# Half-width rotation tables and coefficients folded into them, in a fused state-space and MLP kernel

## The chip, the cores and the metric

The kernel runs on one core of a Trainium2 chip. The metric is device time in microseconds (us) of one execution. Below, PE is the matmul engine, PEld its weight load, DVE the vector engine, ACT the scalar engine, POOL the general-purpose engine and SP the engine that issues most DMAs. All profiled executions named here were of state fast.

## The reference, cut to what matters

The input x is 2048 rows of 1024. Two branches are computed from it and mixed by a gate per row:

```
g = sigmoid((x * gate_w).sum(-1))
# branch a: a diagonal complex state-space model with 1024 states
Lam_bar = exp(dt * Lam);  B_bar = ((Lam_bar - 1) / Lam)[:, None] * B
Bu = x @ B_bar^T
h[t] = Lam_bar * h[t-1] + Bu[t]          # 2048 steps
a = 2 * real(h @ C^T) + x * Dskip
# branch b: layer norm, 1024 -> 3584, gelu, 3584 -> 1024
out = g * a + (1 - g) * b
```

## The kernel before: the parts that matter

The rows come in 8 chunks of TP = 256; the states in 8 groups of 128. For each chunk and state group there is one *scan unit*, 64 in all. PE makes z = B x (L777). DVE rotates z by -theta*j ("pre"), runs two real scans with the decay r, and rotates back by +theta*j ("post"). With the rotation taken out, the complex recurrence is two real ones. The tables cos(theta*j) and sin(theta*j) are 256 wide, built once; j counts from 0 in each chunk, and the state is rotated by theta*256 between chunks.

```python
def s_unit_dve(c, pc):                      # A, B, Cv, Dv, E: fp32 tiles of 128x256
    # pre: six tensor_tensors, A = zre*cos + zim*sin, Cv = zim*cos - zre*sin
    tensor_tensor_scan(A, rb, A, init_re, mult, add)
    tensor_tensor_scan(Cv, rb, Cv, init_im, mult, add)
    # post: six tensor_tensors, h_re = A*cos - Cv*sin, h_im = A*sin + Cv*cos, to bf16
```

The factor (Lam_bar-1)/Lam of B_bar is a complex number per state. The kernel before multiplies it into C, while it transposes C by PE in 16 blocks during the first chunk:

```python
def tc_block(pc, dh):
    ...  # 8 PE transposes into one PSUM bank: creT, cimT
    K.op("act", ... activation(kt0, cimT, Identity, scale=k1b))
    K.op("act", ... activation(kt1, cimT, Identity, scale=k2b))
    STT(k1, creT, k1a, kt0, mult, add)      # DVE, 128x512, L459
    STT(k2, creT, k1b, kt1, mult, add)
```

SBUF is the memory that the engines work in, PSUM the one that PE writes to, in banks. STT below is a scalar_tensor_tensor, one DVE instruction that does two operations. w1 and w2 are the weights of the two MLP layers: w1 is loaded by SP, 1 MB at a time, into two buffers; w2 by POOL in eight loads of 0.9 MB, four for each half of its columns. bt is the transposed B.

So there are two stages. In the *start*, chunk 0 goes through its scan units and the first MLP layer in eight rounds; tables are built, B and C transposed, weights loaded. Then each chunk's second MLP layer and output are woven with the next chunk's scan units and first MLP layer (the *steady state*). The first second-layer matmul, L870, marks the border.

## Time and profile before

The time was 709.8 us (median of 4, 708.98 to 711.25). The next fence is the busy time of each engine in four stretches: start and length in us, busy us of each engine (instructions), then the granted PE clock, the DMA share and GB/s.

```profile
20.00:60.00 40.00, 31.50 (x299) 26.79 (x297) 32.05 (x78) 32.86 (x64) 28.66 (x60) 0.85 0.83 264
60.00:95.00 35.00, 23.74 (x229) 19.58 (x230) 32.56 (x73) 27.13 (x47) 6.03 (x12) 0.90 0.86 293
160.00:240.00 80.00, 79.04 (x566) 53.85 (x564) 56.68 (x151) 22.22 (x40) 38.52 (x56) 1.00 0.55 179
240.00:320.00 80.00, 79.03 (x564) 53.66 (x562) 53.18 (x151) 22.67 (x41) 35.16 (x53) 1.00 0.55 180
```

The columns are PE, PEld, DVE, ACT, POOL. In the steady state PE is busy 79 of 80 us and DVE 53 to 57: PE is the limit. In the start, PE is busy 31.5 of 40 and 23.7 of 35 us; from 60 to 95 us DVE is busy 32.6 of 35.

The chain of waits of the first 112 us, by line, names DVE first:

```profile
by line: DVE ct L459 16.7%; DVE vt L442 12.8%; issue 6.2%; PE psF L777 6.1%; DMA arena<-in_A_log_dt_dram 5.0%; PE psF L835 4.7%; DVE vt L461 3.2%; ACT arena L767 2.7%; PE psF L870 2.6%; ACT arena L769 2.6%; POOL arena L452 2.5%; DVE vt L803
```

DVE's timeline around one scan unit shows costs (start us, duration us, instruction):

```profile
61.42 1.40 DVE L459 SCALAR_TENSOR_TENSOR ct<-psF,cs,arena 128x512 bf16<-128x512 bf16 x2
62.74 1.40 DVE L459 SCALAR_TENSOR_TENSOR ct<-psT,cs,arena 128x512 bf16<-128x512 bf16 x2
64.06 0.41 DVE L442 TENSOR_TENSOR vt<-psF,tabc 128x256 f32<-128x256 f32 x1
...
65.38 0.75 DVE L442 TENSOR_TENSOR vt<-vt 128x256 f32<-128x256 f32 x2
66.05 0.75 DVE L803 TENSOR_TENSOR_SCAN vt<-cs,vt 128x256 f32<-128x256 f32 x1
66.71 0.73 DVE L805 TENSOR_TENSOR_SCAN vt<-cs,vt 128x256 f32<-128x256 f32 x1
67.35 0.40 DVE L442 TENSOR_TENSOR vt<-vt,tabc 128x256 f32<-128x256 f32 x1
```

Recorded durations overlap, so costs are read from start to start. An STT takes 0.66 us ((64.06 - 61.42)/4), a scan 0.66 us, a tensor_tensor 0.33 us. The pre part begins at 64.06, the scans at 66.05, the post part at 67.35: the scans take 1.30 us.

### The profile page before, as it was taken

To read this page: it belongs to the slowest core of one execution; us is meant where nothing else is said; L and a number is where in the kernel's file an instruction comes from. 1 tells how busy PE (TensorE), PEld (TensorE's weight loads), DVE (VectorE), ACT (ScalarE), POOL (GpSimd) and SP (SyncE) were. 2 spreads that over 40 slices of the span, in tenths; PEclk is the share of its full clock that TensorE was granted. 3 is DMA by queue.
4 is the path that set the end of the run, shared out by engine and by line. 5 is a ranking of instruction groups with operands and counts; after the bars stand their busy time and mean duration, and the time that the engine had idled before them with its cause. 6 is when DMAs were issued, how large, how long until landed. Compare 5 with 4: busy or idle time off the path is not lost.

```text
span 709.4 us, 12210 instructions
## 1 busy us (share of the span) xinstructions
PE 658.6 (93%) x4738; PEld 449.2 (63%) x4738; DVE 459.9 (65%) x1228; ACT 234.0 (33%) x416; POOL 331.2 (47%) x509
## 2 busy tenths in 40 slices
PE   4878669999999999999999999999999999999994
PEld 3666546666666666666666666666666666666541
DVE  3789896777677666575677667575677666555300
ACT  6787962222322232212312232222312232211100
POOL 5681343655353644354353643364353642443573
PEclk9889998999999999999999999999999999999998
DMA  7786989466554646356554656355554655462220
GB/s 267 253 282 207 322 287 329 157 190 208 179 168 140 228 152 220 133 183 204 179 182 136 216 168 212 129 191 194 178 194 136 212 174 170 144 190 91 60 51 16
DMA packets 84627, 130.04 MB, mean 183 GB/s; under 512 B 4890, under 2 KB 66330, under 8 KB 84570
## 3 DMA queue, kind: packets, MB, share of 16 engines
q1 hardware_dynamic: 76330, 104.88, 45.1%
q0 software_dynamic: 8240, 24.39, 10.9%
q8 instruction: 37, 0.61, 0.4%
q14 instruction: 20, 0.16, 0.1%
HBM read 120.86 MB, written 8.39 MB: 182 GB/s over the span
## 4 chain that ended last, share of the span: by engine, by line
PE 82%; DVE 7%; ACT 5%; POOL 2%; issue 1%; DMA 1%; DVEq 0%; POOLq 0%; ACTq 0%
PE psF L870 27%; PE psF L835 25%; PE psF L885 15%; PE psF L777 15%; DVE ct L459 3%; DVE vt L442 2%; ACT xT L714 2%; DMA arena<-in_A_log_dt_dram 1%; PE psT L711 1%; ACT hid L838 1%; DVE vt L461 1%; ACT arena L767 0%; ACT arena L769 0%; POOL arena L452 0%; DVE vt L803 0%
## 5 line engine op out<-in xcount | busy, mean ns | idle before, releaser
L835 PE MATMUL psF<-yT,w1s 128*128 128x256 bf16 x1792 | 235.0, 276 | 5.7 <-ACT hid L838 3.0
L835 PEld LDWEIGHTS psF<-yT,w1s 128*128 128x128 bf16 x1792 | 176.6, 99 | 64.6 <-ACT hid L838 4.1
L442 POOL TENSOR_TENSOR arena<-arena 128x512 f32<-128x512 f32 (+1 forms) x96 | 120.0, 1250 | 143.3 <-ACT arena L877 101.1
L442 DVE TENSOR_TENSOR vt<-psF,tabc 128x256 f32<-128x256 f32 x128 | 53.6, 419 | 182.3 <-PE psF L777 180.3
L777 PE MATMUL psF<-xT,bts 128*128 128x256 bf16 x1024 | 129.7, 276 | 1.7 <-ACT bts L733 1.1
L838 ACT ACTIVATE arena<-psF,b1c 128x256 bf16<-128x256 f32 x112 | 53.1, 474 | 226.8 <-PE psF L835 226.8
L777 PEld LDWEIGHTS psF<-xT,bts 128*128 128x128 bf16 x1024 | 100.9, 99 | 27.8 <-ACT bts L733 1.5
L870 PE MATMUL psF<-w2s,hid 128*128 128x512 bf16 x448 | 110.6, 381 | 1.5 <-ACT xT L714 1.5
L838 ACT ACTIVATE hid<-psF,b1c 128x256 bf16<-128x256 f32 x112 | 52.0, 478 | 170.4 <-PE psF L835 170.4
L870 PE MATMUL psF<-w2s,arena 128*128 128x512 bf16 x448 | 107.1, 379 | 0.0
L870 PEld LDWEIGHTS psF<-w2s,arena 128*128 128x128 bf16 x448 | 43.7, 98 | 39.8
L870 PEld LDWEIGHTS psF<-w2s,hid 128*128 128x128 bf16 x448 | 43.8, 98 | 37.6 <-ACT xT L714 1.6
L885 PE MATMUL psF<-ct,hT 128*128 128x512 bf16 x256 | 63.1, 379 | 0.0
L452 POOL TENSOR_SCALAR lnf<-lnf 128x1 f32<-128x1 f32 x32 | 17.5, 547 | 96.9 <-DVE lnf L678 95.2
L885 PE MATMUL psF<-ct,arena 128*128 128x512 bf16 x256 | 61.8, 379 | 0.0
L896 POOL DMA_DIRECT2D out_dram<-arena x32 | 17.5, 548 | 93.2 <-DVE arena L459 65.4
L442 DVE TENSOR_TENSOR vt<-vt,tabc 128x256 f32<-128x256 f32 x128 | 53.9, 421 | 0.0
L442 DVE TENSOR_TENSOR vt<-psF,tabs 128x256 f32<-128x256 f32 x128 | 53.1, 415 | 0.0
L442 DVE TENSOR_TENSOR vt<-vt 128x256 f32<-128x256 f32 x128 | 52.5, 452 | 0.0
L442 DVE TENSOR_TENSOR vt<-vt,tabs 128x256 f32<-128x256 f32 x128 | 49.9, 431 | 0.0
L803 DVE TENSOR_TENSOR_SCAN vt<-cs,vt 128x256 f32<-128x256 f32 x64 | 49.3, 771 | 0.0
L459 DVE SCALAR_TENSOR_TENSOR arena<-psF,gall,arena 128x512 bf16<-128x512 f32 x32 | 23.9, 746 | 37.0 <-PE psF L885 35.6
(111 smaller groups left out, 647.0 us busy)
## 6 DMA issues: line engine op xcount, KB each, us to landing
w1s<-in_B_w_dram SPq DMA_DIRECT2D x56, 1024.0 KB, 5.8
bts<-bt_scratch SPq DMA_DIRECT2D x56, 512.0 KB, 3.6
w2s<-in_B_w_dram POOLq DMA_DIRECT2D x8, 896.0 KB, 10.0
xn<-in_A_x_dram SPq DMA_DIRECT2D x16, 256.0 KB, 6.1
bt_scratch<-bts SPq DMA_DIRECT2D x8, 512.0 KB, 3.2
arena<-in_A_x_dram POOLq DMA_DIRECT2D x32, 128.0 KB, 3.7
arena<-in_A_Dskip_dram POOLq DMA_DIRECT2D x32, 128.0 KB, 3.8
arena<-in_B_b_dram POOLq DMA_DIRECT2D x32, 128.0 KB, 3.9
```

The source lines that it names most:

```text
L442: K.op(eng, lambda e: e.tensor_tensor(out_, a, b, op), reads=r, writes=w, name=name, after=after)
L452: K.op(eng, lambda e: e.tensor_scalar(out_, a, s1, s2, op0, op1), reads=r, writes=w, name=name, after=after)
L459: K.op(eng, lambda e: e.scalar_tensor_tensor(out_, a, s, b, op0, op1), reads=r, writes=w, name=name, after=after)
L461: K.op(eng, lambda e: e.scalar_tensor_tensor(out_, a, s, b, op0, op1, accum_out=accum), reads=r, writes=w, name=name, after=after)
L714: K.op("act", lambda e: e.activation(dst[:, :, s * TB:(s + 1) * TB], bap[:, 0:NDC, :], AF.Identity), reads=[bkey], writes=[dkey], name="tr ...
L777: K.op("pe", lambda e, ri=ri, dc=dc: e.matmul(psF[:, PZ, ri * TP:(ri + 1) * TP], bts[:, slot, dc, ri * 128:(ri + 1) * 128], xT[:, dc, :], ...
L803: K.op("dve", lambda e: e.tensor_tensor_scan(A, rb, A, Cc("init_re", pc), ALU.mult, ALU.add), reads=[kv(VA), kc("r"), kc("init_re")], writ ...
L835: K.op("pe", lambda e, dc=dc: e.matmul(psF[:, ab, 0:TP], w1s[:, slot, dc, fl * 128:(fl + 1) * 128], yT[:, dc, :], start=(dc == 0), stop=(d ...
L838: K.op("act", lambda e: e.activation(hid[hb][:, fc, :], psF[:, ab, 0:TP], AF.Gelu_apprx_tanh, bias=b1c[:, fc:fc + 1]), reads=[kps(ab), ("b ...
L870: K.op("pe", lambda e, fc=fc: e.matmul(psF[:, PM, 0:DH], hid[hb][:, fc, tbl * TB:(tbl + 1) * TB], w2s[:, fc, dh * DH:(dh + 1) * DH], start ...
L885: K.op("pe", lambda e, k=k: e.matmul(psF[:, PS_, 0:DH], hT[hb][:, k, tbl * TB:(tbl + 1) * TB], ct[:, k, dh * DH:(dh + 1) * DH], start=(k = ...
L896: K.dma("pool", lambda e: e.dma_start(out2[tbg * TB:(tbg + 1) * TB, dh * DH:(dh + 1) * DH], ost[:, 0, :]), reads=[("ost", 0)], name="out_s ...
```

## The change

Its intent: multiply the factor not into C but into the post tables (16 tables of 128 columns instead of scaling 16 blocks of C), so that C needs plain copies only. The post tables need room. So the tables shrink to T = 128, used twice per chunk by a stride-0 dimension; the scan is split in two, and the state is rotated by theta*128 at the join. The coefficients are now needed before the first unit ends, so their computation moves forward. Two DMA issues move too: the first-half w2 loads, all in the fifth round before, go one each into rounds 2 to 5, and the reloads of transposed B (bt prefetch) go to the end of a round.

```diff
-    T = TP
+    T = 128
+    NF = TP // T
@@ scan unit
+            for f in range(NF):
+                ... scan a_f, scan c_f, each 128 wide
+                if f + 1 < NF:          # four 128x1 operations on DVE
+                    TS("dve", t1, c_l, sT, mult);  TS("dve", t2, c_l, cT, mult)
+                    STT(mre, a_l, cT, t1, mult, subtract);  STT(mim, a_l, sT, t2, mult, add)
-            TT("dve", B, A, tc_, ALU.mult, ...)        # post with the plain tables
+            TT("dve", B, A, pcn, ALU.mult, ...)        # post with tables that hold the factor
@@ C blocks
-            two ACTIVATEs with scale, two STTs
+            two plain copies of 128x512: even blocks on ACT, odd ones on DVE
@@ new
+        def ptable(pc, eng):            # POOL: six 128x128 operations for each group
+            tpc = k1a*cos + k1b*sin;  tpn = k2b*sin + k1b*cos
@@ order
+        consts_dve_2(); consts_act(); coef_chain()     # moved ahead of the first unit
+            if 1 <= rnd < 1 + NW2G:
+                w2_load(rnd - 1, 0)                    # POOL queue, before the round's ptable
+            for pcc in fin_batches.get(rnd, []):
+                ptable(pcc, "pool")
+            if rnd == 0:
+                for pc in pool_tabs[2:]:
+                    table_pool_args(pc)                # arguments of tables 4 to 7
-            if rnd == w2a_round:                       # round 5 (counting from 1)
-                for g in range(NW2G):
-                    w2_load(g, 0)
+            if pcn < NPC:
+                bt_prefetch(pcn + 3)                   # was right after s_unit_dve
```

## The prediction

> **What bounds it now.** The kernel has two stages. The 40-slice page shows PE at 9 tenths from slice 7 on; the busy-by-stretch table gives PE 79.04 of every 80 us between 160 and 640 us. There one 256-row chunk takes 79.5 us and is PE-bound; DVE is busy 54 of 80 us, off the critical path. The start, up to the first second-layer matmul (L870) at 104.56 us, is different: between 20 and 106 us PE is busy 61.9, ACT 66.6, DVE 75.4 of 86 us, and from 38 us DVE hardly idles. The chain of waits walks there mostly over DVE: the C-coefficient STTs (L459, 16.7% of the first 112 us) and the scan unit's tensor_tensors (L442, 12.8%).
>
> **What the change removes.** In the start only: 32 STTs of 128x512 (0.66 us from start to start, 21 us) on DVE and 32 scaling ACTIVATEs (0.57 us, 18 us), as the coefficients move from C into the "post" tables. 128-wide tables also halve table elements on ACT and POOL.
>
> **What it adds.** 32 plain copies, half on ACT (about 0.57 us each, 9 us), half on DVE. For these I estimate 0.35 to 0.65 us, 6 to 10 us: the Trainium skill's "VectorE: DVE Perf Modes", section "The perf-mode tier table", allows a PSUM copy up to 2x, which no run so far shows. POOL builds 8 post tables, 6 operations of 128x128 each, about 2 us by its 0.41 to 0.73 us for 128x256. In each of the 64 scan units two 256-wide scans (0.66 us) become four 128-wide ones (estimate 0.36 us) plus four 128x1 rotations in a dependent chain (0.07 to 0.2 us each, by the other tiny DVE operations): about +0.8 us a unit, 5.6 to 6.4 us. The stride-0 table operands I take as free (0.33 us per tensor_tensor as now).
>
> **What lies on the critical path.** Steady state: DVE rises from 54 to about 60 of 80 us, still below PE; expected cost about 0. Start: DVE net -21 + 8 + 6.4, some -6 us, and the waits of DVE for ACT (4.98 us at 33 us, 0.85, 1.5) mostly go. The coefficient chain moves ahead of the first table: the second layer norm waits for POOL, so the first unit's end and the second table come 2 to 3 us later; but the third unit starts about 36 to 37 us instead of 42.2. Following the rounds, the last unit of chunk 0 begins about 88 us instead of 99.8. Earlier w2 loads and the later bt prefetch also take a 2.6 us w1 wait of PE at 92 us away. Against it: DMA, busy 0.85 of 20 to 106 us at 278 GB/s, must deliver the same bytes sooner, and ACT becomes nearly as busy as DVE. I discount to a gain of 11 us, all before the first L870.
>
> **Time:** 698.5 us, range 691 to 705. Faster by over 2% 0.28, within 2% 0.68, slower 0.04.
>
> **What would show it.** First L870 matmul at about 93 us (90 to 99) instead of 104.6; from there to the end unchanged, about 605 us, chunk period 79.5 us; DVE in 240 to 320 us at 59 to 62 us instead of 53; 128-wide scans at 0.45 us recorded or less; third unit's first "pre" near 37 us; PE waits for DVE (L459) inside the start gone.
>
> **What would make it wrong.** Scans or rotations costing so much that DVE nears 80 us a chunk (then slower); broadcast operands running slower; the early coefficient chain delaying the first MLP matmuls by more than 4 us; DMA or ACT table loads (1.28 us, two per second round) becoming the limit of the start (gain 4 us or less); or, the other way, PE becoming the limit and the gain reaching 15 us or more.

## The result

The kernel after takes 700.46 us (median of 10, 699.59 to 701.45); the kernel before 710.05 us (median of 15). The ratio is 0.9865, 95% interval 0.9852 to 0.9878. Ratios here are the mean time of one kernel's fast runs over that of the other's fast runs of the same rounds, so they are not quite the ratios of the medians quoted.

The same four stretches after:

```profile
20.00:60.00 40.00, 34.55 (x362) 29.48 (x362) 32.43 (x99) 33.42 (x61) 30.79 (x73) 0.92 0.88 297
60.00:95.00 35.00, 24.26 (x244) 20.97 (x242) 31.20 (x90) 20.45 (x40) 22.97 (x52) 0.90 1.01 342
160.00:240.00 80.00, 79.03 (x564) 53.65 (x562) 65.46 (x197) 22.65 (x41) 36.76 (x55) 1.00 0.58 182
240.00:320.00 80.00, 79.04 (x565) 53.79 (x564) 65.51 (x198) 22.26 (x41) 35.51 (x53) 1.00 0.57 178
```

PE in the steady state is unchanged; DVE rose from 53 to 65.5 us and stays under PE. From 60 to 95 us POOL's work went from 6 to 23 us and the DMA share from 0.86 to 1.01.

The border of the stages, from PE's timeline, first before and then after:

```profile
104.56 1.89 PE L870 MATMUL psF<-w2s,hid 128*128 128x512 bf16 x4 [1.48 <-ACT xT L714]
```

```profile
94.94 1.89 PE L918 MATMUL psF<-w2s,hid 128*128 128x512 bf16 x4 [1.48 <-ACT xT L742]
```

The start became 9.6 us shorter (104.56 - 94.94). From there to the end of the span it takes 604.8 us before (709.4 - 104.56) and 603.6 after (698.5 - 94.94), and the transposes that end each chunk come 79.51 us apart in both traces. The gain lies in the start.

DVE's timeline around one unit after, with the same columns as before:

```profile
68.84 0.74 DVE L795 COPY ct<-psF 128x512 bf16<-128x512 bf16 x2
69.51 0.74 DVE L795 COPY ct<-psT 128x512 bf16<-128x512 bf16 x2
70.17 0.41 DVE L445 TENSOR_TENSOR vt<-psF,tabc 128x256 f32<-128x256 f32 x1
...
72.16 0.48 DVE L840 TENSOR_TENSOR_SCAN vt<-cs,vt 128x128 f32<-128x128 f32 x1
72.55 0.46 DVE L842 TENSOR_TENSOR_SCAN vt<-cs,vt 128x128 f32<-128x128 f32 x1
73.04 0.34 DVE L453 TENSOR_SCALAR mfx<-vt,cs 128x1 f32<-128x1 f32 x2
73.30 0.34 DVE L462 SCALAR_TENSOR_TENSOR mfx<-vt,cs,mfx 128x1 f32<-128x1 f32 x2
73.67 0.48 DVE L840 TENSOR_TENSOR_SCAN vt<-cs,mfx,vt 128x128 f32<-128x128 f32 x1
74.08 0.46 DVE L842 TENSOR_TENSOR_SCAN vt<-cs,mfx,vt 128x128 f32<-128x128 f32 x1
74.45 0.40 DVE L445 TENSOR_TENSOR vt<-vt,tpc 128x256 f32<-128x256 f32 x1
```

A copy takes 0.33 us ((70.17 - 68.84)/4) where an STT took 0.66. The scans and the join take 2.29 us (74.45 - 72.16) where they took 1.30: 1.0 us more a unit. The broadcast table operand is free: 0.33 us from start to start as before.

The chain of waits of the first 112 us no longer names the STTs; it names a w1 load:

```profile
by line: DMA w1s<-in_B_w_dram 10.3%; DVE vt L445 7.6%; ACT bts L761 6.6%; PE psF L918 6.3%; PE psF L883 5.6%; POOL cs L445 5.4%; issue 4.5%; ACT hid L886 4.1%; DMA arena<-in_A_log_dt_dram 3.9%; PE psF L801 3.7%; DVE vt L464 3.3%; ACT L886 2
```

This is a single load, issued at 34.11 us and landed 11.56 us later. It is not new: in the kernel before, one issued at 33.95 took 11.81 us, and was not on the chain.

There is a new wait. In the fifth unit DVE stands still until POOL has built that unit's post table. The timeline of 56 to 72 us, cut to the lines that show it:

```profile
58.42 0.29 POOL L455 TENSOR_SCALAR tabc<-tabc 128x128 f32<-128x128 f32 x1
58.66 1.96 POOL L537 DMA_DIRECT2D w2s<-in_B_w_dram  x2
60.66 0.38 POOL L455 TENSOR_SCALAR arena<-tabc,cs 128x128 f32<-128x128 f32 x1
...
62.82 0.45 POOL L445 TENSOR_TENSOR tpn<-arena 128x128 f32<-128x128 f32 x1
63.38 0.42 DVE L445 TENSOR_TENSOR vt<-vt,tpc 128x256 f32<-128x256 f32 x1 [5.30 <-POOL tpn L445]
...
69.73 1.01 PE L758 MATMUL psF<-ident,arena 128*128 128x128 bf16 x8 [5.63 <-DVE ct L795]
```

The brackets give the idle time before an instruction and what ended it. POOL's queue was in order: the arguments of tables 4 to 7, two w2 issues, then the post table of group 4. DVE lost 5.30 us, and PE 5.63 us behind it, because the copies that free the transposes' PSUM banks came late on DVE.

### The profile page after: what moved, and what is told of

It reads as the page before. It is cut to its first block, busy times and chain, and to the rows that moved or that the text cites. A ratio compares the mean times of both kernels' runs of the same rounds, so it can differ in the third digit from the quotient of the medians.

```text
span 698.5 us, 12590 instructions
## 1 busy us (share of the span) xinstructions
PE 654.7 (94%) x4738; PEld 447.4 (64%) x4738; DVE 527.1 (75%) x1596; ACT 220.7 (32%) x400; POOL 338.3 (48%) x557
## 4 chain that ended last, share of the span: by engine, by line
PE 83%; ACT 6%; DVE 4%; POOL 2%; DMA 2%; issue 1%; SPq 1%; POOLq 0%; DVEq 0%; ACTq 0%
PE psF L918 28%; PE psF L883 25%; PE psF L933 15%; PE psF L801 14%; ACT xT L742 2%; DMA w1s<-in_B_w_dram 2%; DVE vt L445 1%; ACT bts L761 1%; POOL cs L445 1%; ACT hid L886 1%; DMA arena<-in_A_log_dt_dram 1%; PE psT L739 1%; DVE vt L464 1%; ACT L886 0%; DVE ct L795 0%
## 5 line engine op out<-in xcount | busy, mean ns | idle before, releaser
L883 PE MATMUL psF<-yT,w1s 128*128 128x256 bf16 x1792 | 231.4, 273 | 3.4 <-ACT hid L886 1.9
L801 PE MATMUL psF<-xT,bts 128*128 128x256 bf16 x1024 | 131.4, 279 | 0.3 <-ACT bts L761 0.3
L445 DVE TENSOR_TENSOR vt<-vt 128x256 f32<-128x256 f32 x128 | 71.6, 600 | 0.0
L455 POOL TENSOR_SCALAR lnf<-lnf 128x1 f32<-128x1 f32 x32 | 17.4, 543 | 89.1 <-DVE lnf L706 87.5
L445 DVE TENSOR_TENSOR vt<-vt,tpc 128x256 f32<-128x256 f32 x128 | 53.6, 419 | 6.1 <-POOL tpn L445 6.1
L445 DVE TENSOR_TENSOR vt<-vt,tpn 128x256 f32<-128x256 f32 x128 | 48.8, 423 | 0.0
L455 POOL TENSOR_SCALAR arena<-arena,gall 128x512 f32<-128x512 bf16 x64 | 45.9, 723 | 2.4 <-DMA arena<-in_B_b_dram 2.4
```

The source lines that it names most:

```text
L445: K.op(eng, lambda e: e.tensor_tensor(out_, a, b, op), reads=r, writes=w, name=name, after=after)
L455: K.op(eng, lambda e: e.tensor_scalar(out_, a, s1, s2, op0, op1), reads=r, writes=w, name=name, after=after)
L801: K.op("pe", lambda e, ri=ri, dc=dc: e.matmul(psF[:, PZ, ri * TP:(ri + 1) * TP], bts[:, slot, dc, ri * 128:(ri + 1) * 128], xT[:, dc, :], ...
L883: K.op("pe", lambda e, dc=dc: e.matmul(psF[:, ab, 0:TP], w1s[:, slot, dc, fl * 128:(fl + 1) * 128], yT[:, dc, :], start=(dc == 0), stop=(d ...
```

## The experiments

The theory with which they began: the start is bound by DVE's work, folding takes 21 us of STTs out of it, the split costs 1.0 us in each of its 8 units, and the moved DMA issues are a detail. The rivals: the narrower tables give the gain; the moved DMA issues give it; something other than DVE sets the start's pace.

Twelve kernels ran. Two of them, fold_only and pool_first_fold, leave out the rotation at the join and so are wrong (they serve for timing and say nothing of the result); w2_double loads one matrix twice and is still correct, like all others. The table below collects the times. "Before" of each row is the kernel before in the same rounds.

| kernel | us, median | before, us | ratio, 95% interval | first second-layer matmul, us | from there to the end, us |
|---|---|---|---|---|---|
| before | 709.8 | | | 104.56 | 604.8 |
| after | 700.46 | 710.05 | 0.9865 (0.9852 to 0.9878) | 94.94 | 603.6 |
| split_only | 708.2 | 709.0 | 0.9982 (0.9957 to 1.0008) | 101.59 | 604.6 |
| fold_only | 701.11 | 709.0 | 0.9887 (0.9858 to 0.9915) | 96.39 | 604.0 |
| old_order | 707.7 | 709.0 | 0.9982 (0.9951 to 1.0013) | 93.74 | 610.6 |
| new_order | 710.05 | 709.0 | 1.0013 (0.9986 to 1.0041) | 103.51 | 604.4 |
| split_new_order | 708.7 | 709.38 | 0.9986 (0.9971 to 1.0001) | 102.37 | 602.9 |
| pool_first | 698.88 | 709.38 | 0.9854 (0.9837 to 0.9870) | 92.41 | 602.9 |
| pool_first_ln | 700.94 | 709.38 | 0.9876 (0.9850 to 0.9902) | 92.62 | 607.1 |
| pool_first_fold | 698.03 | 709.38 | 0.9841 (0.9826 to 0.9856) | 93.34 | 604.1 |
| w2_early | 696.94 | 710.3 | 0.9804 (0.9789 to 0.9819) | 92.68 | 602.0 |
| w2_early_ln | 698.0 | 710.3 | 0.9833 (0.9808 to 0.9857) | 91.69 | 603.8 |
| w2_double | 704.74 | 710.3 | 0.9917 (0.9902 to 0.9932) | 99.71 | 603.1 |
| tile_64 | 775.88 | 710.3 | 1.0898 (1.0864 to 1.0932) | 98.49 | 676.2 |

The last two columns come from one profiled execution each (the last is span minus the column before it). Its first unit begins anywhere from 14.69 us (new_order) to 18.55 us (w2_double), so one or two us in the border are chance.

### split_only: the half-width tables and split scans without the folding

```diff
 (to the kernel before)
+ T = 128, NF = 2; split scans with the join; consts_dve_2 and consts_act ahead of the first table
  C is still scaled by 2 ACTIVATEs and 2 STTs a block; w2 loads and bt prefetch as before
```

> The kernel before with 128-wide tables and split scans (the sines of the constants are computed earlier, as the split needs), but with C still scaled by 32 ACTIVATEs and 32 STTs. Theory (the gain comes from the DVE work that folding the coefficients removes from the start; the split is a cost that only the PE-bound part hides): 8 units in the start longer by 1.0 us each, against a little saved by narrower tables on POOL and ACT: 713 to 718 us, first second-layer matmul at 107 to 112 us. Rival A (the narrower tables and earlier constants bring the gain): 700 to 706 us. DVE busy in 240 to 320 us: 60 to 66 us, as in the kernel after.

It is neither the theory's 713 to 718 nor the rival's 700 to 706: 708.2 us, a ratio of 0.9982 whose interval includes 1. The trace says why. The third unit begins at 36.93 us instead of 42.18, exactly where it begins in the kernel after: narrower tables and earlier constants, which were not run apart, do pay 5 us in the first third of the start. But from the third unit to the eighth it takes 59.5 us (96.39 - 36.93), against 57.6 before (99.76 - 42.18) and 53.2 after (90.15 - 36.93). So this edit is not a pure cost in the start, as the theory had it; what the tables and constants save there about pays for the split. DVE in 240 to 320 us was 64.98 us, as expected.

### fold_only: the change without the split (wrong result)

```diff
 (to the kernel after)
- for f in range(NF): scans of 128, join of four 128x1 operations
+ one scan of 256 for each part, no rotation at the join
```

> The kernel after with one 256-wide scan for each part and no rotation at the join: a wrong result on purpose, the same reads, writes and order otherwise. Theory: what the split costs in the start is 1.0 us a unit, but the fifth unit waits for POOL in the kernel after, so only the three units behind that wait count: 3 us less than after, 696 to 699 us; DVE busy in 240 to 320 us 8 us less than after or more. Rival (the split costs the start nothing, since other engines set its pace): the same as after within 1 us, 699.5 to 701.5 us. Second rival (DVE is what the whole start waits for): 8 us less, about 692 us.

701.11 us: the same as the kernel after, as the first rival said, not 696 to 699 and not 692. DVE did get its time back (in 240 to 320 us it is busy 53.39 us instead of 65.51), and it was worth nothing: the fifth unit now waits 6.99 us for POOL's post table instead of 5.30. The theory that DVE's work sets the pace of the changed start fell here.

### old_order and new_order: the two DMA moves alone

```diff
 old_order (to the kernel after)
- w2_load one a round in rounds 2 to 5; bt_prefetch at the end of a round
+ w2_load four times in round 5; bt_prefetch right after s_unit_dve
 new_order (to the kernel before)
+ the reverse
```

> The kernel after with w2 loads all in the fifth round and the bt prefetch ahead of the MLP matmuls, as in the kernel before. Theory (folding is the gain): 699 to 703 us; the POOL wait before the fifth unit's post part shrinks by about 2 us, because two w2 issues of 0.98 us no longer stand before its post table. Rival B (the reordering of DMA issues is the gain): 706 us or more.

> The kernel before with the DMA issues reordered as in the kernel after (w2 loads spread over rounds 2 to 5, bt prefetch at the end of a round), nothing else. Theory: 707 to 710 us, at most the 2.6 us w1 wait less. Rival B: 703 us or less.

This was the surprise. new_order gives nothing (710.05 us, at the upper end of the theory's 707 to 710). But old_order gives 707.7 us, far outside the theory's 699 to 703 and in rival B's range: without the moves, the rest of the change gains nothing that its interval can tell from 0. The wait for POOL in the fifth unit shrank by more than the 2 us expected, from 5.30 to 0.82 us, and the border comes at 93.74 us. Then this happens (from the timeline of 80 to 106 us):

```profile
80.36 3.85 POOL L537 DMA_DIRECT2D w2s<-in_B_w_dram  x4
...
82.95 4.78 SPq L497 DMA_DIRECT2D w1s<-in_B_w_dram  x2
92.46 3.85 POOL L537 DMA_DIRECT2D w2s<-in_B_w_dram  x4
...
102.45 1.89 PE L883 MATMUL psF<-yT,w1s 128*128 128x256 bf16 x8 [5.51 <-DMA w1s<-in_B_w_dram]
```

The chain of waits puts the whole time between into one transfer:

```profile
82.95 19.45 DMA w1s<-in_B_w_dram
```

In the kernel before the same four w2 issues went out at 73.91 us, 31 us ahead of the border. In old_order they stand in POOL's queue behind the post tables of groups 6 and 7, go out at 80.36, and the border is only 13 us away. The second four follow at 92.46, and a w1 load that shares the DMA engines with all of them lands after 19.45 us. In the kernel after the first four w2 loads have landed by 82.13 us, and the two w1 loads issued next (84.07 and 88.82) take 6.8 and 6.7 us; the median over that whole kernel is 5.9. The Trainium skill's "DMA: Bandwidth & Descriptors", section "Queues, rings and completion order", says that each DMA engine takes turns between its queues, so a load on SP is not served ahead of loads on POOL; the trace agrees. This is the DMA view of old_order from 98 to 102 us, when both queues have work (queue: packets, MB, share; q1 is SP's, q0 POOL's: w2_early, which moves 2.7 MB of loads from POOL to SP, has 5.25 MB on q0 in the first 110 us where the kernel after has 7.96):

```profile
q0 software_dynamic: 288, 1.11, 80.8%
q1 hardware_dynamic: 285, 0.28, 24.1%
```

The two queues move packets one for one, but those of w2 are four times as large (1.11 MB in 288, against 0.28 MB in 285), so SP's loads get a fifth of the bytes. Which of the two moves matters was not run apart; the trace points to the w2 loads.

### split_new_order: everything but the folding

```diff
 (to split_only)
+ the DMA moves of new_order
```

> split_only with the DMA issues in the new order: everything of the change but the folding of the coefficients. Theory now (folding shortens the start's compute, and the new DMA order lets the transfers keep up; each alone gives nothing): 706 to 709 us, with the start still set by the STTs on DVE. Rival (split and order are enough, folding gives nothing): 699 to 702 us.

708.7 us, within the theory's range. Together with the runs above this makes a square, all four with split scans and half-width tables:

| | old DMA order | new DMA order |
|---|---|---|
| C scaled (not folded) | 708.2 (split_only) | 708.7 (split_new_order) |
| folded into the post tables | 707.7 (old_order) | 700.46 (after) |

Neither folding nor order gains anything that the intervals tell from 0 alone; together they gain about 8 us. Folding here includes what it needs on POOL, the earlier coefficients and the new order of the tables. Folding lets the engines reach the border sooner; only the new order has the weights there by then.

### pool_first: the new wait on POOL taken away

```diff
 (to the kernel after)
  round 1: arguments of tables 4 and 5 only
  round 3: post tables of 4 and 5, then the arguments of 6 and 7, then the w2 issue
```

> The kernel after with POOL's queue in another order: the post tables of chunks 4 and 5 stand before the table arguments of 6 and 7 and before that round's w2 issue. Theory (the fifth unit's 5.3 us wait for POOL is a new wait of the change, and it sets the start's pace): that wait goes under 1.5 us, first second-layer matmul at 90 to 92 us instead of 94.9, 695.5 to 698 us. Rival (DMA sets the pace, busy 1.01 of 60 to 95 us in the kernel after): 699.5 to 701 us, the saved time comes back as PE waits for w1 loads.

The wait is gone: DVE waits for no POOL table between 30 and 100 us, and the fifth unit's successor begins at 66.73 us instead of 70.17. The time is 698.88 us and the border 92.41, both just above the theory's ranges, the time below the rival's; its interval (0.9837 to 0.9870) overlaps that of the kernel after. Of 5.3 us of wait, some 1.6 us by the medians, or 0.8 by the ratios, came back as time, and by the intervals it may be none. PE waited 2.34 us for a w1 load at 82.93 us, where the kernel after waits 1.04: part of it turned into a DMA wait, as the rival said.

### pool_first_fold: pool_first without the split (wrong result)

```diff
 (to pool_first)
+ the edit of fold_only
```

> pool_first without the split scans (wrong result on purpose, as in fold_only). In fold_only the split's 1.0 us a unit was hidden behind POOL; if it is DVE's turn once POOL is out of the way: 3 to 6 us less than pool_first. If DMA or the other engines set the pace: the same within 1 us.

698.03 us, within 1 us of pool_first. But POOL is not out of the way here: DVE, now faster, waits for post tables again (4.2 us in all from 30 to 100 us, 3.45 in one wait), and for PE 8.8 us instead of 5.3. So the split's 8 us are hidden once more; that DVE sets the pace in pool_first, where it is busy 34.03 of 35 us from 60 to 95, is not excluded.

### pool_first_ln: an earlier layer norm for the next chunk

```diff
 (to pool_first)
- the next chunk's layer norm in rounds 6 and 7
+ in rounds 5 and 6
```

> The same, and the layer norm of the next chunk one round earlier, so that PE does not wait for it at the end of the start. If compute order is what is left: 3 us less than pool_first. If DMA is the limit: the same as pool_first.

700.94 us, no gain. The layer norm, now ahead on DVE, makes PE wait 6.10 us for a unit at 81.53 us. The border is where it was (92.62), and the first woven chunk then waits 2.56 us for a w1 load at 110.06 us; from the border to the end it takes 607.1 us.

### w2_double: more to load (unneeded data)

```diff
 (to the kernel after)
+ in rounds 2 to 5 one more load of 0.9 MB each, into unused memory, last on SP's queue
```

> The kernel after with 3.7 MB of extra loads into unused memory in rounds 2 to 5 of the start, issued on SP behind that round's other issues; the result is right. At the 342 GB/s of 60 to 95 us they take 10.7 us. If DMA limits the start: 707 to 712 us, most of the gain of the change gone. If it has slack there: 700 to 703 us.

704.74 us: 4.3 us more than the kernel after, between the two expectations. The extra 10.7 us of transfer are neither free nor paid in full. PE now waits 3.88 us at 83.43 us for a w1 load. DMA limits some of the start, not all of it. The extra loads stand in SP's own queue ahead of the next w1 load, so the run does not separate shared bandwidth from the order in that queue.

### w2_early and w2_early_ln: loads moved into the idle stretch

The kernel after leaves DMA idle early. Its DMA view of the first 110 us (40 slices of 2.75 us, busy tenths and GB/s) shows the hole at 16 to 22 us:

```profile
DMA  2999960089999999998791999999999999899999
GB/s 81 295 348 378 377 242 0 0 271 314 371 382 338 360 359 338 352 369 276 239 330 28 188 337 387 350 358 365 391 379 400 324 341 334 265 288 322 366 375 345
```

```diff
 w2_early (to pool_first)
+ after the third B load: w2_load(0..2, 0) on the SP queue;  only the fourth stays in round 5
 w2_early_ln
+ also the edit of pool_first_ln
```

> pool_first with three of the four first-half w2 loads (2.7 MB) issued on the SP queue right after the third B load, in the stretch from about 13 us in which the kernel after moves hardly any bytes (0 to 2 GB/s in two slices of 3.1 us). Theory (the same bytes must pass before the second layer starts, and DMA, busy 0.99 to 1.01 of 60 to 95 us, is what limits the start once POOL is out of the way): first second-layer matmul at 87 to 90 us, PE waits for w1 loads shorter, 693 to 696.5 us. Rival (the engines' order limits): 698 to 700 us, as pool_first; or worse, since the C loads at 23 us come behind these loads.

> The same with the next chunk's layer norm one round earlier. If DMA held pool_first_ln back: 1 to 4 us less than w2_early. If the earlier layer norm is bad in itself (it stands before the seventh unit on DVE): 1 to 2 us more.

The hole is filled:

```profile
DMA  3999999999999999999787199968299999999999
GB/s 84 279 321 381 324 314 285 341 369 368 325 360 394 367 351 361 374 339 322 232 307 241 42 317 356 350 182 287 83 283 341 348 377 359 309 352 349 368 357 343
```

w2_early takes 696.94 us, ratio 0.9804 (0.9789 to 0.9819). This beats both kernels: its interval lies clear of that of the kernel after. The time came 0.4 us above the theory's range, and not all went as expected: the border came at 92.68 us, not at 87 to 90, although from 66 us on PE waits for no w1 load in the start. What PE waits for then is the next chunk's layer norm (2.47 and 1.90 us for ACT's yn), and w2_early_ln shows that moving this earlier does not help either (698.0 us, its interval overlaps; PE then waits 6.09 us for DVE at 81.20). The stretch of 60 to 95 us of w2_early, in the columns used before:

```profile
60.00:95.00 35.00, 27.18 (x279) 22.77 (x280) 34.52 (x104) 24.95 (x45) 26.86 (x60) 0.92 0.83 274
```

The DMA share is down to 0.83 and DVE is busy 34.52 of 35 us. This points to DVE as the limit once more; no run tested it, so what limits the start at 92 us is left open.

### tile_64: how much room the steady state has

```diff
 (to the kernel after)
- T = 128
+ T = 64
```

> The kernel after with scans of 64: eight scans and three joins a unit. From 0.66 us for 256 and 0.40 for 128 (start to start) 0.27 us for 64, and 0.64 us a join: about 1.9 us more a unit, 15 us a chunk, DVE at about 80 of 80 us. Theory (DVE off the critical path as long as it stays under PE's 79.5 us a chunk): at the edge, chunk period 79.5 to 84 us, 701 to 730 us in all. Rival (steady state has ample slack): 699 to 702 us.

775.88 us, worse than either side expected. In a unit beside which POOL does little, a scan of 64 takes 0.26 us from start to start and the scans with three joins 4.29 us (300.36 to 304.65), 2.0 more than with 128: the estimate of 1.9 was right for such a unit. That makes 16 us more a chunk, but the chunk grew by more. The stretch of 240 to 320 us, in the columns used before (PE, PE weight load, DVE, ACT and POOL busy after the length):

```profile
240.00:320.00 80.00, 73.01 (x508) 48.51 (x505) 78.17 (x257) 21.08 (x38) 36.28 (x52) 0.98 0.53 170
```

And PE's waits for DVE in 240 to 640 us (waiting engine, tile and line, what ended the wait; us in all, times, the longest in us):

```profile
PE psF L801 <- DVE vt L445: 35.0, 15, 3.3
```

DVE is busy 78.2 of 80 us, and chunks come 89.6 us apart on average ((632.92 - 184.98)/5) instead of 79.51. PE waits for the units' PSUM bank, 35.0 us in 400, because DVE is now the limit. Its work is 87.5 us a chunk (468.79 us of the 480 from 160 to 640, times 89.6), where it was 63.6 with T = 128 (384.04 of 480, times 79.51): 24 us more, not 16. The other 8 us lie in disturbed units: the scans and joins of the next unit took 6.25 us (310.82 to 317.07) while POOL did two 128x512 scalings and two adds (309.57 to 314.2). Why such units cost more was not tested apart. The rival (ample slack) fell: with T = 128 DVE has 16 us left in each 80, and 24 more do not fit.

## Why the prediction was right, point by point

- **Time.** 698.5 was said, 700.46 came, inside the range of 691 to 705 and the likeliest class (within 2%). A gain of 11 us was said, 9.6 came.
- **Where.** The border was said to be at 93 us (90 to 99): 94.94. The rest was said to be unchanged at about 605 us: 603.6. The third unit was said to begin near 37 us: 36.93. The last unit "about 88 us instead of 99.8": 90.15. All this held in the trace.
- **"Expected cost about 0" in the steady state** held, but DVE's size was off. The prediction said 59 to 62 us for 240 to 320 us; it was 65.5 (64.0 of 80 on average from 160 to 640). Two terms were mis-sized. The split costs 1.0 us a unit, not 0.8 (a 128-wide scan takes 0.40 us, not 0.36; the join 0.64 us): 8 us a chunk. Most of the rest is in the pre part's two adds, both inputs in SBUF, which recorded 629 ns on average against 444 before and 432 in fold_only: 3 us for the 16 of a chunk. split_only has it too (633), so it comes with the split and not with the folding. One pair took 2.20 us at 238.30 us, while POOL did its two 128x512 scalings and an add (237.46 to 240.2); 9.5 us later, with POOL idle or issuing, it took 0.75. The Trainium skill's "SBUF — State Buffer", section "Who interferes with whom", says that a DVE instruction with two SBUF inputs contends with a POOL instruction that reads SBUF; the trace agrees. That the longer unit meets POOL's work more often is a reading of these traces; no run tested it.
- **"PE waits for DVE (L459) inside the start gone"** was wrong as a prediction of PE's waits: the STTs went, and one wait of 5.63 us for DVE's copy took their place. It came from a queue that the prediction had not followed to its end, that of POOL. It had counted "about 2 us" for each post table, and not what stands ahead of it.
- **The copies** were put at 0.35 to 0.65 us and took 0.33. The skill's "VectorE: DVE Perf Modes", section "The perf-mode tier table", which allows a copy from PSUM up to 2x, agrees with this: 512 bf16 elements in 0.33 us are 1.6 elements a ns, twice the rate of the STT (512 in 0.66 us).
- **The step that failed though the number was right** is the sum on DVE: "DVE net -21 + 8 + 6.4". It treats the start as DVE-bound on both sides of the change. The profile before agrees for the old side. In the kernel after the +6.4 is hidden (fold_only: same time without it, DVE waits longer instead), and POOL's queue and DMA hold part of the start. **The DMA moves were costed at a 2.6 us wait**; without them the change gains some 1.3 us (old_order, ratio 0.9982, with 1 inside its interval) instead of 9.6. The gain belongs to folding and moves together, and the sum has no such term. That 11 us was said and 9.6 came rests on a discount made by judgement, and is in part luck. The discount's reason, "against it: DMA … must deliver the same bytes sooner", named the right opponent without a number. w2_double puts one on it: 10.7 us of extra transfer cost 4.3 us.

## What to carry to other kernels

When a start-up phase is limited by one engine, taking that engine's work away moves the limit to whatever must then arrive sooner. Here the gain existed only with the weight loads moved too, and neither edit would have looked worth keeping alone. Before adding work to an idle engine's in-order queue, list what already stands in that queue ahead of it and what will stand behind it: here a table waited behind other tables' arguments, and in old_order weight loads waited behind tables. Work that is hidden under another limit is not free: with T = 128 the scan split cost the steady state nothing, and with T = 64 it cost 9% of the whole.

## What the Trainium skill lacked or had wrong

- "DVE: opcode table, instruction layouts, handler registers and perf-mode slots", section "Datapath and trigger behaviour", says that the built-in scan runs at half throughput. The runs agree: going from 128 to 256 elements adds 0.26 us, 2.0 ns an element, where an STT of 128x1024 takes 1.10 us from start to start (86.51 to 87.61 us in the kernel after), 1.07 ns an element. It does not give the fixed cost of a scan, which decides how small a scan may be: 0.13 us from start to start (0.26 for 64 elements, 0.40 for 128, 0.66 for 256).
- No page consulted gives the cost of a short chain of dependent 128x1 operations on DVE; it belongs to "Vector Engine (DVE) Microarchitecture Reference", section "Measured stream behaviour on trn2": the four of the join took 0.63 us from the first one's start to the next scan's start (73.04 to 73.67).
- "SBUF — State Buffer", section "Who interferes with whom", states which instructions contend but gives no size for two-input fp32 operations: here a pair of 128x256 adds went from 0.75 to 2.20 us beside POOL's 128x512 work.
- "DMA: Bandwidth & Descriptors", section "Queues, rings and completion order", says that queues take turns. It gives no size for what a latency-critical load loses: here a 1 MB load took 19.45 us beside up to eight loads of 0.9 MB, against 6.7 and 6.8 us without them. SP's packets were served one for one with POOL's, but with 1 KB packets against 4 KB it got a fifth of the bytes (0.28 of 1.39 MB from 98 to 102 us).
